# Fourier layer and maxout MLP on one core: batch 0's complex product as three float32 products, with the rows of v moved block by block and their product two groups behind

## The chip, the cores and the metric

The kernel runs on one core of one Trainium2 chip. The metric is the device time of one launch in microseconds (us), the median of several runs. Engine names are those of the profile: PE is TensorE's matmuls, PEld its weight loads, DVE is VectorE, ACT is ScalarE, POOL is GpSimd, SP is the sync engine, which here only issues transfers. An engine runs its instructions strictly in the order in which they were put on it.

## The reference

`x` is 8 batches of 3072 rows by 256 columns, float32. What must be computed, cut to what matters:

```python
X = np.fft.rfft(x, axis=1)                      # along the 3072 rows of a batch
Yr = X.real @ w_r - X.imag @ w_i + b_r          # the complex product, w_r, w_i: 256 x 256
Yi = X.real @ w_i + X.imag @ w_r + b_i
Yr = sign(Yr) * maximum(abs(Yr) - 0.01, 0)      # soft threshold, the same for Yi
y = np.fft.irfft(Yr + 1j * Yi, n=3072, axis=1)
h = maximum(maximum(y @ w1, y @ w2), y @ w3)    # 256 -> 768
out = h @ w_out                                 # 768 -> 256
```

The weights of the MLP come in as float64.

## The kernel before

A transform of 3072 points is split as 96 times 32. Stage A multiplies by a 96-point table and goes through memory (`a_d`); from there on the frequencies are taken in 12 groups (`NJP = 12`) of 128 rows and two blocks `j`. Per group k three steps on PE follow each other: `stage_b` (32-point table, tile `px`, transposed result copied to `tf`), `stage_w` (the complex product with w_r and w_i, tile `py`, result `u` with bias and soft threshold) and `stage_q` (the 32-point inverse table, tile `pz`, whose copy `zs` goes to memory as `z_d`). The last part of the inverse transform reads `z_d` back, and its result feeds the MLP, which is most of the run: 8 batches of 8 chunks, six `up`/`down` steps each.

Batches 1 to 7 run their three stages spread between the MLP's steps of the batch before. Batch 0 has no MLP to hide behind: it runs alone, before the first `up`, in plain float32, through `first_b` (line 655), `first_w` (line 682) and `first_q` (line 713). A float32 matmul shows in the trace as two instructions.

In `first_w` the rows of a group hold real and imaginary part as two halves of 64, so `tf` holds for each block the transposed pair and, in front of it, the imaginary half again with its sign turned (lines 669 and 672, two ACT copies). Each output block needs two products for each half of the 256 contracted columns: eight float32 matmuls of 128x256 a group (lines 691 and 692). Then DVE adds the bias (line 696), ACT makes two rectified copies (lines 701 and 702) and DVE subtracts them (line 703). `first_q` (line 718) takes `u` as it lies. In the loop over k (from line 1151) iteration k issues the load of group k+3, `stage_b` of k+1, `stage_w` of k and `stage_q` of k-1.

```python
for fn, i in (
    (load_a, k + 3), (stage_b, k + 1), (stage_w, k), (finish_w, k), (stage_q, k - 1),
):
```

Into the same iterations a hand-written plan (from line 1127) puts the MLP's weights: loads on SP (lines 354 and 358), and the conversion from float64 bits to two float16 halves, which is DVE and ACT work (lines 363, 390 to 409, 136 and 137). After group 11 the exponent of the largest value is taken (line 265 and on), five more float32 tiles of batch 1's stage A run on PE (line 592), `z_d` is read back (line 956), and `first_inverse` and the first `up` follow. The framework orders each engine's instructions when the program is built, by the order of the program and by when it takes operands to be ready; the order is fixed after that.

SP's queue carries the group loads (`aj`, line 629), all weights, tables and inputs; ACT's queue carries the `z_d` stores (line 894). PSUM tiles of this part come from eight banks in turn (`ff_tile`). `uf` has three buffers, `aq` two, `xm` one.

Of the kernel before, what the change touches and what calls it, by code (L numbers as in the profile page):

```python
# [101 lines left out]
def fourier_maxout_kernel(  # L102
    ctx: ExitStack, tc: tile.TileContext, x, w_r, w_i, b_r, b_i, w1, w2, w3, w_out, fa, ga, mb, mq, ident, out
):
    nc = tc.nc
# [128 lines left out]

    def load_fft_weights():
        ws = raw_tile("wst").rearrange("p (k c) -> p k c", k=KD)
        for i, w in enumerate((w_r, w_i)):
            nc.sync.dma_start(
                out=ws[:, :, i * D:i * D + D], in_=w.rearrange("(k p) d -> p k d", p=P)
            )  # L240
        return [ws[:, kd] for kd in range(KD)]

    def load_tables():
        rows = [b.rearrange("(r o d) -> r o d", r=1, o=1) for b in (b_r, b_i)]
        for c in range(2):
            nc.sync.dma_start(out=bias[64 * c:64 * c + 64, 0:1], in_=rows[c].broadcast_to([64, 1, D]))
        nc.sync.dma_start(out=qf, in_=mq[:, 0:2])
        nc.sync.dma_start(out=id_sb, in_=ident)
        st["tiled"] = s_tile("tiled")[:, 0:P]
        nc.sync.dma_start(out=st["tiled"], in_=mq[:, 26])  # L250

    def load_last_bias():
        rows = [b.rearrange("(r o d) -> r o d", r=1, o=1) for b in (b_r, b_i)]
        for c in range(2):
            nc.sync.dma_start(out=bias[64 * c:64 * c + 64, 1:2], in_=rows[c].broadcast_to([64, 1, D]))
        nc.gpsimd.dma_start(out=bias[96:97, 1:2], in_=rows[0])
# [53 lines left out]
    def scale_bias():  # L310
        mb = small("mxb")
        nc.vector.tensor_reduce(
            out=mb, in_=bias[:, 0], axis=AX.X, op=ALU.max, apply_absolute_value=True
        )
        st["eb"] = small("ebf")
        nc.vector.tensor_scalar(
            out=st["eb"], in0=exponent_of(mb, "b", 23, 0xFF, 60.0), scalar1=1.0, scalar2=-37.0,
            op0=ALU.mult, op1=ALU.add,
        )
# [185 lines left out]
    def load_m(q):  # L505
        b, q4 = divmod(q, NCH)
        xv = x[b].rearrange("(n1 n2) d -> n1 n2 d", n2=N2)[:, q4 * NQ:(q4 + 1) * NQ, :]
        with tc.issue_after(st["ld"].ins):
            st["m", q] = xm = fft.tile([N1, NQ * D], F32, name="xm", bufs=1)
            nc.sync.dma_start(out=xm.rearrange("p (n d) -> p n d", n=NQ), in_=xv)  # L510
# [147 lines left out]
    def first_b(k):  # L658
# [8 lines left out]
        st["t", k] = t = fft.tile([P, KD, 384], F32, name="tf", tag="t2", bufs=2)  # L667
        tv = t.rearrange("p h (j m) -> p (h j) m", j=2)
# [12 lines left out]

    def first_w(k):
        last = k == NJP - 1
# [3 lines left out]
        for j in range(2):  # L687
# [12 lines left out]
        t = fft.tile([P, 2, D], F32, name="t", bufs=1)  # L700
        nc.scalar.activation(out=t, in_=u, func=AF.Relu, bias=mlam)
        nc.scalar.activation(out=u, in_=u, func=AF.Relu, scale=-1.0, bias=mlam)
        nc.vector.tensor_tensor_reduce(
            out=u, in0=u, in1=t, scale=1.0, scalar=0.0, op0=ALU.subtract, op1=ALU.max,
            accum_out=mx[:, NJP + k:NJP + k + 1],
        )
# [4 lines left out]
        st["u", k] = u  # L711

    def first_q(k):
        u = st.pop(("v", k))
        pz = ff_tile("pz")
# [436 lines left out]
    for k in range(-3, NJP + 1):  # L1152
        for fn, i in (
            (load_a, k + 3), (stage_b, k + 1), (stage_w, k), (finish_w, k), (stage_q, k - 1),
        ):
            if 0 <= i < NJP:
                if fn == stage_q and i == NJP - 1:
# [4 lines left out]
        with tc.issue_after(st["ld"].ins):  # L1162
# [15 lines left out]
            if k == 6:  # L1178
                whole = ga_sb.rearrange("p i e n m -> p (i e n m)")
                nc.sync.dma_start(out=whole, in_=ga[:, 0:2 * N2 * N1])  # L1180
                first = fft.tile([N1, NQ * D], F32, name="xm", bufs=1).bitcast(F16)[:, 0:2 * NT]
# [8 lines left out]
    with tc.issue_after(st["late"].ins):  # L1190
        for c, v in enumerate((b_r, b_i)):
            row = v.rearrange("(o d) -> o d", o=1)
            nc.gpsimd.dma_start(out=bias_ri[:, c], in_=row.broadcast_to([P, D]))
# [103 lines left out]
```

## Time and profile before

| | us |
|---|---|
| median of 3 runs | 1980.62 (1979.61 to 1983.82) |
| the profiled execution's own time | 1980.65 |
| its span, first to last instruction | 1978.9 |

The profiled execution stands 0.03 us above the median, so what is worked out from its trace can be set against the median directly; 1.75 us of its time lie around the span. In the rows below, a busy time is the union of an engine's instructions; single durations overlap a little at their ends. A window's columns are its length, and for each engine the busy time and the number of instructions, then the granted share of TensorE's clock (1.00 is 2.4 GHz), the share of the 16 DMA engines in use, and GB/s.

### The profile page before, as it was taken

Reading aid. Unit: us, or ns where it says so; the run is one execution under the profiler, and the core shown is the slowest. Engines: PE = TensorE matmul, PEld = TensorE weight load, DVE = VectorE, ACT = ScalarE, POOL = GpSimd, SP = SyncE. Lnnn points to the kernel's source line nnn. Section 1 sums busy time; section 2 is a strip of 40 time slices with the busy share of each in tenths; the row PEclk is TensorE's granted clock in tenths of the full one; section 3 lists DMA queues with packets and bytes.
Section 4 is the critical chain, followed back from the end, with each engine's and each line's share of the span. In section 5 each row is a group of like instructions: output and inputs, shape, how many; then the busy total and the mean of one; then the engine's idle time right before and its main releaser. Section 6 shows DMA issues by size and latency. Waiting matters only on the chain.

```text
span 1978.9 us, 44328 instructions
## 1 busy us (share of the span) xinstructions
PE 1961.3 (99%) x16839; PEld 1355.9 (69%) x16839; DVE 1521.3 (77%) x3159; ACT 1064.3 (54%) x2186; POOL 280.5 (14%) x510
## 2 busy tenths in 40 slices
PE   9989999999999999999999999999999999999999
PEld 5746776676766766666766676666676677766666
DVE  3788887888877988778887888868887687765554
ACT  5755664566545565456554565545655455443343
POOL 1001111111111122111121021111122001100000
PEclk9999999999999999999999999999999999999999
DMA  8756564565545564555555465544552344221111
GB/s 291 212 150 172 157 163 124 156 174 154 145 133 163 143 189 115 151 150 161 159 137 149 133 186 145 147 139 130 149 154 73 90 115 123 68 76 49 49 49 33
DMA packets 201843, 269.75 MB, mean 136 GB/s; under 512 B 30846, under 2 KB 149982, under 8 KB 201534
## 3 DMA queue, kind: packets, MB, share of 16 engines
q1 hardware_dynamic: 168830, 191.37, 36.7%
q0 software_dynamic: 25168, 68.59, 10.7%
q10 hardware_dynamic: 7632, 6.95, 1.2%
q8 instruction: 133, 2.18, 0.5%
q14 instruction: 80, 0.66, 0.1%
HBM read 124.31 MB, written 75.50 MB: 101 GB/s over the span
## 4 chain that ended last, share of the span: by engine, by line
PE 93%; DVE 3%; DMA 2%; ACT 1%; issue 1%; SPq 0%; ACTq 0%; DVEq 0%
PE pu L179 19%; PE pu L181 18%; PE pu L180 18%; PE pd L181 6%; PE pd L180 6%; PE pd L179 6%; PE py L179 3%; PE py L180 3%; PE py L181 3%; PE pi L1021 2%; PE px L737 2%; PE pa L575 2%; PE pz L905 1%; PE pa L592 1%; PE py L692 0%
## 5 line engine op out<-in xcount | busy, mean ns | idle before, releaser
L179 PE MATMUL pu<-yh,wuh 128*128 128x384 f16 x2304 | 752.2, 327 | 2.6 <-DVE h L1062 1.7
L181 PE MATMUL pu<-yh,wul 128*128 128x384 f16 x2304 | 751.5, 326 | 0.0
L180 PE MATMUL pu<-yl,wuh 128*128 128x384 f16 x2304 | 751.5, 326 | 0.0
L173 ACT ACTIVATE hh<-h 128x384 f16<-128x384 f32 x384 | 200.2, 521 | 432.3 <-DVE h L1062 428.4
L181 PEld LDWEIGHTS <-wul 128*128 128x128 f16 x2304 | 225.5, 98 | 149.7 <-issue 0.9
L179 PEld LDWEIGHTS <-wuh 128*128 128x128 f16 x2304 | 225.3, 98 | 145.1 <-issue 34.2
L181 PE MATMUL pd<-woh,hh 128*128 128x256 f16 x1152 | 313.4, 273 | 0.7 <-DVE hh L174 0.7
L180 PE MATMUL pd<-wol,hh 128*128 128x256 f16 x1152 | 313.8, 273 | 0.0
L179 PE MATMUL pd<-woh,hh 128*128 128x256 f16 x1152 | 313.8, 273 | 0.0
L180 PEld LDWEIGHTS <-wuh 128*128 128x128 f16 x2304 | 225.5, 98 | 116.1 <-issue 5.0
L174 DVE SCALAR_TENSOR_TENSOR hh<-h,hh 128x384 f16<-128x384 f32 x384 | 213.3, 555 | 108.3 <-ACT hh L173 105.4
L1059 DVE TENSOR_TENSOR c<-pu,c 128x384 f32<-128x384 f32 x384 | 212.1, 552 | 95.8 <-PE pu L181 90.3
L1056 ACT ACTIVATE c<-pu 128x384 f32<-128x384 f32 x384 | 186.7, 486 | 139.9 <-PE pu L181 136.8
L1062 DVE TENSOR_TENSOR h<-pu,c 128x384 f32<-128x384 f32 x384 | 211.7, 551 | 29.2 <-PE pu L181 24.8
L1093 POOL DMA_DIRECT2D out_dram<-o x189 | 104.7, 559 | 581.3 <-ACT o L1091 569.7
L585 POOL DMA_DIRECT2D a_d<-aq x160 | 94.0, 591 | 612.4 <-ACT aq L582 590.0
L181 PE MATMUL py<-wch,tt 128*128 128x256 f16 x504 | 137.3, 273 | 0.0
L179 PE MATMUL py<-wch,tt 128*128 128x256 f16 x504 | 137.3, 272 | 0.0
L180 PE MATMUL py<-wcl,tt 128*128 128x256 f16 x504 | 137.3, 272 | 0.0
L179 PEld LDWEIGHTS <-hh 128*128 128x128 f16 x1152 | 112.7, 98 | 33.5
L180 PEld LDWEIGHTS <-hh 128*128 128x128 f16 x1152 | 112.7, 98 | 33.4
L181 PEld LDWEIGHTS <-hh 128*128 128x128 f16 x1152 | 112.7, 98 | 15.2 <-DVE hh L174 1.9
(236 smaller groups left out, 2659.3 us busy)
## 6 DMA issues: line engine op xcount, KB each, us to landing
zq<-z_d SPq DMA_DIRECT2D x63, 384.0 KB, 4.8
out_dram<-o POOLq DMA_DIRECT2D x189, 128.0 KB, 3.3
ab<-a_d SPq DMA_DIRECT2D x84, 256.0 KB, 4.1
ab<-ab SPq DMA_DIRECT2D x336, 64.0 KB, 3.0
vb<-vb SPq DMA_DIRECT2D x308, 64.0 KB, 2.9
z_d<-zs POOLq DMA_DIRECT2D x70, 256.0 KB, 3.8
xm<-in_x_dram SPq DMA_DIRECT2D x40, 384.0 KB, 3.5
a_d<-aq POOLq DMA_DIRECT2D x160, 96.0 KB, 2.9
```

The source lines that it names most:

```text
L173: nc.scalar.activation(out=hi, in_=src, func=AF.Copy, scale=scale)
L174: later(lambda: low(nc.vector.scalar_tensor_tensor(out=lo, in0=src, scalar=scale, in1=h, op0=ALU.mult, op1=ALU.subtract)))
L179: nc.tensor.matmul(o, lh, rh, start=start, stop=False, **kw)
L180: nc.tensor.matmul(o, lh, rl, start=False, stop=False, **kw)
L181: st["mm"] = nc.tensor.matmul(o, ll, rh, start=False, stop=stop, **kw)
L575: st["mm"] = nc.tensor.matmul(pa[r][64 * h:64 * h + 64], ft[rows, t], xt[rows, i, h], start=t == i, stop=t == 1,)
L585: nc.gpsimd.dma_start(out=av[1 - r, :, :, n:n + 512], in_=o[64 * h:64 * h + 48])
L737: nc.tensor.matmul(pv[:, h, :, g // 2, g % 2], ah[:, g // 2, g % 2, h * P:(h + 1) * P], mb_sb[:, i, 4 * kb + g].rearrange("p (c m) -> p c ...
L1056: st["act"] = nc.scalar.activation(out=c1, in_=p, func=AF.Copy)
L1059: st["dve"] = nc.vector.tensor_tensor(out=c1, in0=p, in1=c1, op=ALU.max)
L1062: st["dve"] = nc.vector.tensor_tensor(out=h32, in0=p, in1=st["c1"], op=ALU.max)
L1093: q.dma_start(out=out_v[b, c, t], in_=o)
```

## The change

For groups 0 to 10 of batch 0 the complex product is formed from three products: (r + i) w_r, i times -(w_r + w_i), and r times (w_i - w_r), where the first is shared by both parts of the result. The weight sums are formed once by four DVE instructions. The copies from `px` gather the real parts of both blocks into one 128-column stretch and the imaginary ones into another, DVE adds the two, and six matmuls of 128x256 follow. The result then has all 128 rows of both blocks' real part in one half and the imaginary part in the other, so the bias is added by two DVE instructions (the shared product and bias first, the rest second), and the rows have to be moved back to the layout that `first_q`'s table wants: four transfers of 64 rows by 1 KB a group on SP's queue, into half of an `aq` tile. `stage_q` runs two groups behind `stage_w` rather than one, and groups 10 and 11 both after the loop's last product. Group 11 stays as it was. The bias tile of the later batches (`bias_ri`) is loaded at the start on SP's queue (it was loaded by two POOL transfers at the end), and `xm` becomes 128 rows high, with the weight sums in columns that the table part stored there later does not use.

```diff
+    spare_x = fft.tile([P, NQ * D], F32, name="xm", bufs=1)
+    sums = spare_x[:, 2 * D:4 * D].rearrange("p (k d) -> p k d", k=KD)
+
+    def sum_fft_weights(ws):
+        for kd, t in enumerate(ws):
+            r, i, s = (t[:, n * D:n * D + D] for n in range(3))
+            nc.vector.scalar_tensor_tensor(
+                out=sums[:, kd], in0=r, scalar=-1.0, in1=i, op0=ALU.mult, op1=ALU.subtract
+            )
+            nc.vector.tensor_tensor(out=s, in0=i, in1=r, op=ALU.subtract)
...
@@ load_tables
-            nc.sync.dma_start(out=bias[64 * c:64 * c + 64, 0:1], in_=rows[c].broadcast_to([64, 1, D]))
+            nc.sync.dma_start(out=bias_ri[:, c:c + 1], in_=rows[c].broadcast_to([P, 1, D]))
@@ load_last_bias
-            nc.sync.dma_start(out=bias[64 * c:64 * c + 64, 1:2], in_=rows[c].broadcast_to([64, 1, D]))
+            nc.sync.dma_start(out=bias[64 * c:64 * c + 64], in_=rows[c].broadcast_to([64, 2, D]))
@@ scale_bias
-            out=mb, in_=bias[:, 0], axis=AX.X, op=ALU.max, apply_absolute_value=True
+            out=mb, in_=bias_ri.rearrange("p c d -> p (c d)"), axis=AX.X, op=ALU.max, apply_absolute_value=True
@@ first_b, after tf is taken
+        if k < NJP - 1:
+            pc = px.rearrange("p (h j c m) -> p h c j m", h=KD, j=2, c=2)
+            for c in range(2):
+                nc.scalar.activation(
+                    out=t[:, :, c * P:c * P + P].rearrange("p h (j m) -> p h j m", j=2), in_=pc[:, :, c],
+                    func=AF.Copy,
+                )
+            nc.vector.tensor_tensor(
+                out=t[:, :, 2 * P:3 * P], in0=t[:, :, 0:P], in1=t[:, :, P:2 * P], op=ALU.add
+            )
+            return
...
+    def quick_w(k):
+        t = st.pop(("t", k))
+        mx = batch(0, "u")
+        both = [ff_tile("py") for _ in range(2)]
+        for o, part, w in (
+            (both[0][:, 0:D], 2, [v[:, 0:D] for v in fft_weights]),
+            (both[1][:, 0:D], 1, [sums[:, h] for h in range(KD)]),
+            (both[1][:, D:2 * D], 0, [v[:, 2 * D:3 * D] for v in fft_weights]),
+        ):
+            for h in range(KD):
+                nc.tensor.matmul(
+                    o, t[:, h, part * P:(part + 1) * P], w[h], start=h == 0, stop=h == KD - 1
+                )
+        u = fft.tile([P, 2, D], F32, name="uf", tag="vh", bufs=3)
+        nc.vector.tensor_tensor(
+            out=u, in0=both[0][:, 0:D].rearrange("p (o d) -> p o d", o=1).broadcast_to([P, 2, D]),
+            in1=bias_ri, op=ALU.add,
+        )
+        nc.vector.tensor_tensor_reduce(
+            out=u, in0=both[1].rearrange("p (c d) -> p c d", c=2), in1=u, scale=1.0, scalar=0.0,
+            op0=ALU.add, op1=ALU.max, accum_out=mx[:, k:k + 1],
+        )
+        first_threshold(k, u)
+        if k % 2 == 0:
+            st["moved"] = fft.tile([P, NQ * D], F32, name="aq", bufs=2)
+        st["mv", k] = moved = st["moved"][:, k % 2 * 512:k % 2 * 512 + 512].rearrange("p (j d) -> p j d", j=2)
+        for c in range(2):
+            for j in range(2):
+                nc.sync.dma_start(out=moved[64 * c:64 * c + 64, j], in_=u[64 * j:64 * j + 64, c])
...
     def first_w(k):
+        if k < NJP - 1:
+            return quick_w(k)
...
     def first_q(k):
         u = st.pop(("v", k))
+        u = st.pop(("mv", k), u)
...
-            (load_a, k + 3), (stage_b, k + 1), (stage_w, k), (finish_w, k), (stage_q, k - 1),
+            (load_a, k + 3), (stage_b, k + 1), (stage_w, k), (finish_w, k), (stage_q, k - 2),
+            (stage_q, NJP - 1 if k == NJP else -1),
         ):
             if 0 <= i < NJP:
+                if fn == stage_w and i == 0:
+                    sum_fft_weights(fft_weights)
...
-    with tc.issue_after(st["late"].ins):
-        for c, v in enumerate((b_r, b_i)):
-            row = v.rearrange("(o d) -> o d", o=1)
-            nc.gpsimd.dma_start(out=bias_ri[:, c], in_=row.broadcast_to([P, D]))
```

`first_threshold` is the part of `first_w` from line 700 to line 706, made a function of its own.

## Rows read from the trace of the kernel before

**Rows 1.** The page's first part: busy time of each engine over the whole span, its share, and the instructions.

```profile
PE 1961.3 (99%) x16839; PEld 1355.9 (69%) x16839; DVE 1521.3 (77%) x3159; ACT 1064.3 (54%) x2186; POOL 280.5 (14%) x510
```

**Rows 2.** The windows of batch 0's own part and of the first MLP steps (columns as told above).

```profile
29.40:40.00 10.60, 9.59 (x52) 8.01 (x50) 6.92 (x24) 5.57 (x13) 0.00 (x0) 1.00 1.00 347
40.00:70.00 30.00, 29.97 (x153) 24.71 (x153) 28.62 (x64) 22.55 (x39) 0.49 (x1) 1.00 0.95 298
70.00:100.00 30.00, 27.48 (x122) 20.26 (x121) 20.41 (x62) 21.89 (x37) 1.54 (x5) 1.00 0.61 160
100.00:120.00 20.00, 16.90 (x82) 8.68 (x81) 13.49 (x24) 12.64 (x22) 2.67 (x5) 0.83 0.80 244
120.00:150.00 30.00, 26.99 (x194) 16.49 (x192) 29.62 (x61) 14.72 (x29) 0.51 (x1) 1.00 0.29 79
```

**Rows 3.** The timeline of PE over one period of the groups: start, time, instruction, and idle time before it where there was any.

```profile
49.63 0.59 PE L692 MATMUL py<-wst,tf 128*128 128x256 f32 x2
50.06 1.02 PE L718 MATMUL pz<-uf,qf 128*128 128x512 f32 x2
50.92 1.05 PE L664 MATMUL px<-mb_all,aj 128*128 128x128 f32 x8
51.81 0.60 PE L691 MATMUL py<-wst,tf 128*128 128x256 f32 x2
52.25 0.59 PE L692 MATMUL py<-wst,tf 128*128 128x256 f32 x2
...
54.84 0.59 PE L692 MATMUL py<-wst,tf 128*128 128x256 f32 x2
55.27 1.02 PE L718 MATMUL pz<-uf,qf 128*128 128x512 f32 x2
```

**Rows 4.** The timeline of DVE and ACT over what follows the product that ends at 50.2 us.

```profile
50.26 0.69 DVE L696 CUSTOM_DVE_ANT_1 uf<-py,bias 128x512 f32<-128x512 f32 x1 [0.22 <-PE py L692]
50.88 0.08 DVE L696 DVE_READ_ACCUMULATOR2_ANT mxu<- 128x1 f32 x1
51.24 0.72 ACT L701 ACTIVATE t<-uf,mlam 128x512 f32<-128x512 f32 x1
52.33 0.73 ACT L702 ACTIVATE uf<-uf,mlam 128x512 f32<-128x512 f32 x1
53.61 0.68 DVE L703 CUSTOM_DVE_ANT_0 uf<-uf,t 128x512 f32<-128x512 f32 x1
54.22 0.08 DVE L703 DVE_READ_ACCUMULATOR2_ANT mxu<- 128x1 f32 x1
```

**Rows 5.** Groups of like instructions between 27 and 130 us, different shapes apart: busy time, mean ns of one, idle time before.

```profile
L669 ACT ACTIVATE tf<-px 128x512 f32<-128x512 f32 x12 | 7.0, 586 | 14.8 <-PE px L664 11.2 <-DMA rw<-in_moe_w_out_dram 1.8 <-issue 1.0
L672 ACT ACTIVATE tf<-px 128x256 f32<-128x256 f32 x12 | 4.5, 375 | 0.0
L406 DVE SCALAR_TENSOR_TENSOR ru<-ru 128x256 f32<-128x256 uint32 x2 | 0.8, 422 | 0.0
L409 DVE TENSOR_TENSOR ru<-ru,xhl 128x256 f32<-128x256 f32 x2 | 0.8, 422 | 0.0
L312 DVE TENSOR_REDUCE mxb<-bias 128x1 f32<-128x256 f32 x1 | 0.4, 419 | 0.7 <-DMA bias<-in_b_i_dram 0.7
L303 DVE TENSOR_REDUCE mxc<-wst 128x1 f32<-128x512 f32 x2 | 1.3, 680 | 26.3 <-DMA wst<-in_w_i_dram 26.3
```

**Rows 6.** Transfers: three lines of the DMA view of 24 to 100 us (KB each, median us from issue to landing), and of the whole run the 64 KB moves of the later batches, with SP's time for the issue of one (ns, least, median, most).

```profile
rw<-in_moe_w_dram SPq DMA_DIRECT2D x6, 768.0 KB, 8.8
aj<-a_d SPq DMA_DIRECT2D x12, 256.0 KB, 6.3
z_d<-zs ACTq DMA_DIRECT2D x24, 128.0 KB, 3.2
...
vb<-vb SPq DMA_DIRECT2D x308, 64.0 KB, 2.9
...
L864 SPq DMA_DIRECT2D vb<-vb x308: 590/605/1611, 195.5 to 1733.9; - x154
```

**Rows 7.** Waits of PE between 27.2 and 100 us (us in total, times, longest), and the timeline about the longest of them.

```profile
PE pz L718 <- DVE col L265: 1.6, 1, 1.6
PE px L664 <- DMA aj<-a_d: 1.2, 2, 1.0
...
71.78 0.69 DVE L363 TENSOR_REDUCE mwd<-rw 128x2 f32<-128x512 f32 x1 [1.85 <-DMA rw<-in_moe_w_out_dram]
73.22 1.10 PE L718 MATMUL pz<-uf,qf 128*128 128x512 f32 x2 [1.62 <-DVE col L265]
```

**Rows 8.** The timeline from the last group to the first `up`.

```profile
97.33 1.13 PE L721 MATMUL pz<-uf,qf 128*128 128x256 f32 x4 [0.25 <-DVE mxu L703]
98.50 0.60 ACT L890 ACTIVATE zs<-pz 128x512 f32<-128x512 f32 x1 [0.60 <-PE pz L721]
99.12 1.24 ACTq L894 DMA_DIRECT2D z_d<-zs  x2
107.96 0.22 PE L179 MATMUL pi<-xm,zh 96*128 96x96 f16 x1 [2.41 <-ACT zh L173]
110.78 0.80 PE L179 MATMUL pu<-yh,wuh 128*128 128x384 f16 x2 [0.26 <-ACT yh L173]
```

**Rows 9.** Windows of the end of that stretch (columns as in the windows above).

```profile
108.00:110.00 2.00, 1.56 (x21) 1.42 (x22) 1.34 (x2) 0.51 (x1) 0.00 (x0) 0.56 0.68 219
112.00:114.00 2.00, 2.00 (x8) 0.95 (x7) 1.57 (x2) 0.47 (x1) 0.00 (x0) 0.50 0.88 262
115.00:116.00 1.00, 1.00 (x8) 0.57 (x7) 1.00 (x2) 0.00 (x0) 0.00 (x0) 0.97 0.95 324
```

More of the change, by code (lines that the diff above doesn't have):

```diff
@@ L508, in load_m @@
         with tc.issue_after(st["ld"].ins):
-            st["m", q] = xm = fft.tile([N1, NQ * D], F32, name="xm", bufs=1)
+            st["m", q] = xm = fft.tile([P, NQ * D], F32, name="xm", bufs=1)[0:N1]
             nc.sync.dma_start(out=xm.rearrange("p (n d) -> p n d", n=NQ), in_=xv)
@@ L680, in first_b, with first_threshold @@
                 nc.gpsimd.memset(st["ts"][:, :, z:z + 1], 0.0)
+    def quick_w(k):
[27 more added lines that the diff above has]
+                nc.sync.dma_start(out=moved[64 * c:64 * c + 64, j], in_=u[64 * j:64 * j + 64, c])
+    def first_threshold(k, u):
+        t = fft.tile([P, 2, D], F32, name="t", bufs=1)
+        nc.scalar.activation(out=t, in_=u, func=AF.Relu, bias=mlam)
+        nc.scalar.activation(out=u, in_=u, func=AF.Relu, scale=-1.0, bias=mlam)
+        nc.vector.tensor_tensor_reduce(
+            out=u, in0=u, in1=t, scale=1.0, scalar=0.0, op0=ALU.subtract, op1=ALU.max,
+            accum_out=batch(0, "u")[:, NJP + k:NJP + k + 1],
+        )
+        st["u", k] = u
     def first_w(k):
+        if k < NJP - 1:
+            return quick_w(k)
         last = k == NJP - 1
@@ L699, in first_w @@
         )
[L700 to L706, printed above, removed]
+        first_threshold(k, u)
         if last:
@@ L710, in first_w @@
             )
-        st["u", k] = u
     def first_q(k):
         u = st.pop(("v", k))
+        u = st.pop(("mv", k), u)
         pz = ff_tile("pz")
@@ L1180, in fourier_maxout_kernel @@
                 nc.sync.dma_start(out=whole, in_=ga[:, 0:2 * N2 * N1])
-                first = fft.tile([N1, NQ * D], F32, name="xm", bufs=1).bitcast(F16)[:, 0:2 * NT]
+                first = spare_x[0:N1].bitcast(F16)[:, 0:2 * NT]
                 nc.sync.dma_start(out=first, in_=ga[:, 2 * N2 * N1:])
```

## The prediction, on record before the changed kernel ran

> **What bounds the kernel now.** I read the page's busy shares first: PE is busy for 99% of the span [rows 1], so over the whole run only PE's work counts. But the change touches batch 0 alone, so next come the windows of that stretch [rows 2]. From 40 to 70 us PE is busy for 29.97 of 30 us; DVE, however, for 28.62 of the same 30, because the conversion of the MLP's weights shares the stretch. From 70 to 100 PE has 27.48 and DVE only 20.41. So the bound is PE with DVE 5% behind in the first part, and PE alone in the second. Then the timeline of PE [rows 3]: one `first_q` starts at 50.06, the next at 55.27, a period of 5.21 us without a gap; in it the product takes from 51.81 to 55.27, 3.46 us for eight matmuls, 0.43 us each. The waits [rows 7] show what else holds PE between 27 and 100 us: 1.2 us for the load of a group's rows, near the start, and 1.6 us where DVE's order put a reduction of weights that had not landed ahead of the group's work. Last the end [rows 8]: group 11's `first_q` at 97.33 releases the `z_d` round trip, and the first `up` starts at 110.78. What moves 97.33 moves all that follows.
>
> **What the change is worth, part by part.** The sum is made against the profiled execution's own 1980.65 us, which stands 0.03 above the median of 1980.62, so I set it against the median.
>
> PE: two of eight matmuls go, 2 x 0.43 = 0.86 us a group, 9.5 us over 11 groups. The period would be 4.35 us if PE still set it. That is the most that can be gained.
>
> DVE: each group gets an addition of 128x256 in SBUF, 0.42 us by its like [rows 5], and a second 128x512 addition from PSUM, for which I take the first one's 0.69; the next instruction starts 0.62 after it [rows 4], so starts stand some 0.07 closer than the durations, and the two cost 0.97 to 1.11 us a group; I take 0.97, since in a full queue it is starts that count. Eleven groups: 10.7 (12.2). The sums of the weights are four 128x256 instructions, 4 x 0.42 = 1.7, and the reduction of the bias is twice as wide, 0.68 for 0.42, +0.3. In all 12.7 us (14.2) on the engine that already had no room from 40 to 70.
>
> ACT: two copies of 128x256 in place of one of 128x512 and one of 128x256, 2 x 0.375 for 0.586 + 0.375, 0.21 us less a group. ACT is not full (22.55 of 30), so I count nothing; without that cover it would be a gain.
>
> SP and the DMA engines: four issues a group, 0.605 us each [rows 6], 2.4 us of SP a group. They wait for DVE's second threshold instruction, and behind them on SP stand the load of rows three groups ahead and the weights' loads. A group's rows are used three periods later, so I count nothing there; without that distance a late load would cost what the one in rows 7 cost, about 1 us. The bytes, 44 x 64 KB = 2.9 MB, go at 298 to 347 GB/s [rows 2], 8 to 10 us of DMA engines that are 95 to 100% in use until 70 us. What this delays is the weights (rival 3). The biases' load on SP at the start grows by 128 KB (0.4 us of transfer, beside the wait for rows), and two POOL transfers at the end go: nothing. The table part that shares its tile with the sums lies in other columns; I count nothing.
>
> The distance of two groups: from the end of a group's product to its `first_q` there are two periods. What must fit in: bias, threshold and its copies, 50.22 to 54.30 or 4.1 us [rows 3, 4]; four issues, 2.4; the landing, 2.9 us in the later batches, 6.3 for a group's rows in this crowded stretch on the same queue [rows 6]. So 9.4 to 12.8 us against 8.7 at PE's own pace and 10.4 at the old one.
>
> Now the stretch in three parts, since the limits differ.
> - 29.4 to 40 us (groups 0 and 1): DVE has 10.6 - 6.9 = 3.7 us free; it gets 1.7 + 2 x 0.97 = 3.6. No room is left, and PE's saving meets the wait for rows. I count 0, between -1.7 and +0.6.
> - 40 to 70 us: 30 / 5.21 = 5.8 groups. DVE's work becomes 28.6 + 5.8 x 0.97 = 34.2, with the bias 34.5 us; PE's falls to 25. DVE becomes the bound: **+4.5 us** (between -5.0, if the weights' work gives way entirely, and +5.4 by the full durations). The period is then about 6.0 us and the moves, which need 9.4 to 12.8 in two of them, about fit.
> - From 70 us, 3.2 groups of the new kind are left: DVE has 9.6 of 30 us free, gets 3.1, and PE sets the pace again: 3.2 x -0.86 = **-2.8 us** (0 if late weights hold it).
> - The end: group 10's rows come last now. From the end of its product 9.4 us to its `first_q`, where group 11's stands 8.4 behind it (0.86 + 3.46 + 4.1). So +1.0, and group 11's `first_q` comes another 0.86 behind: **+1.9 us**; up to 2.8 if ACT's two stores for group 10, 1.24 us [rows 8], come ahead of group 11's copy.
>
> After that nothing is added or taken. From 120 to 150 us DVE is full (29.62 of 30), so weight work that slips there would cost again, and work that slips into the 6.5 us that DVE is free from 100 to 120 would cost nothing; I count 0, with 2 us either way.
>
> Sum: 0 + 4.5 - 2.8 + 1.9 = +3.6. **Forecast: 1980.6 + 3.6 = 1984.2 us, no gain**: PE's 9.5 us are there, but where most of them fall DVE takes over the bound.
>
> A word on the moves. In this stretch a group's rows on SP's queue land in 6.3 us and the 768 KB weights in 8.8, while ACT's stores of 128 KB land in 3.2 [rows 6]. The Trainium skill (DMA: Bandwidth & Descriptors, "Queues, rings and completion order") says that each issuing engine has a ring of its own on the 16 DMA engines, and that descriptors of one ring are taken in order, those of different rings in turn. The trace agrees: what stands behind the weights is slow, what stands on the other ring is not. By that rule a move is served after all that SP issued before it, which is rival 2.
>
> **The rivals.**
> 1. PE stays the bound, faster. The weights' conversion has no due time before the first `up`; if the order put on DVE lets it slide behind the groups' work, into what is free after 70 us, the period is 4.35 from group 2 on: 9 x -0.86 = -7.7, the end +1.9: -5.8, 1974.8 us. For it: DVE has 3.7 + 1.4 + 9.6 + 6.5 = 21.2 us free from 29.4 to 120 [rows 2], and needs 12.7. Against: the plan issues the conversion ahead of later groups, and the long wait in rows 7 shows that DVE's fixed order does hold PE up. It decides if less than about 1 us of DVE time is added between two products from 40 to 70.
> 2. The moves are late, slower. With 6.3 us of landing the period is 12.8 / 2 = 6.4 until 70: 5.8 x 1.2 = +7.0; from there (4.1 + 2.4 + 2.9) / 2 = 4.7: -1.6; the end +1.9: +7.3, 1987.9 us. With the 8.8 of the weights it is 7.65 and 5.8 x 2.44 = +14.2, 1995 us. For it: the row of the crowded stretch. Against: moves are small, and the loads are ahead of need. It decides when a move takes longer than 12 - 6.5 = 5.5 us, since below that DVE hides it.
> 3. The transfers set the pace of the weights and DVE's order waits for them as at 71.78: PE's saving turns into waiting, DVE's extra work lies beside it, and the change does nothing that can be seen: 1980.6, from -2 to +3.
> 4. The clock falls. After the idle time before 107.96 the granted clock stands at 0.56 and 0.50, the 1.2 GHz level, and is back at 0.97 in the window from 115 [rows 8, 9]. If the idle parts of a DVE-bound period (6.0 - 4.35) did that, a group's PE work would be 8.7 us: 5.8 x 2.7 = +16, 2000 us. Against: the wait of 1.62 us at 71 left the window at 1.00 [rows 2, 7]. The Trainium skill (TensorE: Matmul & The Clock Gate, "Part 1: The HAM clock gate") says that too little activity halves the clock; the trace agrees at 108 us and shows no such fall among the groups.
>
> **Chances.** A difference under 0.2%, 4.0 us, is about what a measurement of this kernel cannot tell from none. The forecast 0.50, its own range 1979 to 1989 (its terms' bounds, without the two that belong to rivals); rival 1 0.20; rival 2 0.18; rival 3 0.08; rival 4 0.04. Below 1976.6: most of rival 1 and a tail of the forecast, 0.18. Above 1984.6: 0.22 of the forecast, 0.16 of rival 2, 0.01 of rival 3, rival 4: 0.43. The rest, 0.39, lies within. The range from 1975 to 1990 leaves out half of rival 1, the late end of rival 2 and rival 4, together under 0.2.
>
> **What would show it.** Right: in the changed trace PE has idle time from 40 to 70 us and its waits there name DVE; the period is near 6 us there and near 4.4 in the last groups; DVE is full until group 11. Wrong: PE full at a period of 4.35 (rival 1); PE waiting in `first_q` for the moved rows (rival 2); waits for weights in DVE's list (rival 3); a granted clock below 1.00 between 30 and 95 us (rival 4). The end is checked by two `first_q` in a row, the first waiting for a move, and by the start of the first `up`: 110.78 + 3.6 = 114.4 us. If that start has moved by the forecast and the time has not, the MLP's first steps gave it back.

## The result, and the profile after

The changed kernel takes 1998.18 us (median of 4 runs, 1997.29 to 1999.45), the kernel before 1981.74 beside it (4 runs): a ratio of 1.0085, 95% interval 1.0069 to 1.0101, so 16 us slower. The forecast was 1984.2 with a range to 1990. The profiled execution took 1997.52 us, its span is 1995.7 (1978.9 before).

The page's first part, and the windows that answer to [rows 2]:

```profile
PE 1962.6 (98%) x16795; PEld 1353.0 (68%) x16795; DVE 1532.0 (77%) x3185; ACT 1064.2 (53%) x2186; POOL 279.4 (14%) x508
```

```profile
29.40:40.00 10.60, 8.74 (x37) 7.32 (x38) 7.79 (x28) 2.92 (x7) 0.00 (x0) 0.84 0.87 306
40.00:70.00 30.00, 24.11 (x97) 18.27 (x96) 24.80 (x53) 17.74 (x32) 0.00 (x0) 0.83 0.76 222
70.00:100.00 30.00, 22.59 (x106) 16.38 (x106) 27.51 (x73) 19.39 (x33) 0.50 (x1) 1.00 0.88 249
100.00:120.00 20.00, 17.39 (x54) 9.75 (x54) 9.87 (x30) 12.46 (x22) 2.06 (x6) 0.91 0.74 218
120.00:150.00 30.00, 24.46 (x168) 14.13 (x166) 23.82 (x45) 16.50 (x31) 1.01 (x2) 0.89 0.58 174
```

No engine is full from 40 to 70 us: PE fell from 29.97 to 24.11, and DVE did not become full but fell too, from 28.62 to 24.80. The DMA engines, at 0.95 before, are at 0.76. The whole stretch waits. From 70 to 100 us DVE is at 27.51 where it was 20.41: weight work that slipped there took the room that was free before. The granted clock stands at 0.84 and 0.83 from 29.4 to 70 us, where it was 1.00, so part of the stretch ran at the 1.2 GHz level. Two of the falls came after PE had waited 2.26 us (until 43.02) and 2.12 us (until 64.39): the clock is 0.50 from 44 to 48 us and 0.53 from 66 to 68 us. Four instructions of a product then took 2.08 us, which take 1.03 at 61.24:

```profile
43.02 2.08 PE L714 MATMUL py<-xm,tf 128*128 128x256 f32 x4 [2.26 <-ACT tf L682]
```

PE's timeline about one `first_q` (answers to [rows 3]; from group 2 to group 11 the period is 6.6 us, before 5.2), then PE's waits from 27.2 to 112 us (answers to [rows 7]; us in total, times, longest):

```profile
57.90 1.06 PE L675 MATMUL px<-mb_all,aj 128*128 128x128 f32 x8
60.31 1.10 PE L776 MATMUL pz<-aq,qf 128*128 128x512 f32 x2 [1.35 <-DMA aq<-uf]
61.24 1.03 PE L714 MATMUL py<-wst,tf 128*128 128x256 f32 x4
64.39 1.16 PE L675 MATMUL px<-mb_all,aj 128*128 128x128 f32 x8 [2.12 <-DMA aj<-a_d]
65.60 1.52 PE L776 MATMUL pz<-aq,qf 128*128 128x512 f32 x2
```

```profile
PE px L675 <- DMA aj<-a_d: 6.8, 7, 2.1
PE py L714 <- ACT tf L682: 4.1, 2, 2.3
PE pz L779 <- DVE mxu L738: 2.6, 1, 2.6
PE py L714 <- DVE xm L241: 2.3, 1, 2.3
PE pz L776 <- DMA aq<-uf: 2.0, 2, 1.4
```

`first_q` (L776) waits for moved rows only 2.0 us in all; the largest entry is the groups' rows from memory, 6.8 us where it was 1.2. DVE and ACT after the product that ends at 57.85 (answers to [rows 4]):

```profile
57.56 0.68 DVE L718 TENSOR_TENSOR uf<-py,bias_ri 128x512 f32<-128x512 f32 x1
60.84 0.68 DVE L722 CUSTOM_DVE_ANT_0 uf<-py,uf 128x512 f32<-128x512 f32 x1
61.94 0.71 ACT L736 ACTIVATE t<-uf,mlam 128x512 f32<-128x512 f32 x1
62.80 0.72 ACT L737 ACTIVATE uf<-uf,mlam 128x512 f32<-128x512 f32 x1
64.51 0.68 DVE L738 CUSTOM_DVE_ANT_0 uf<-uf,t 128x512 f32<-128x512 f32 x1
```

From the product's end to the last subtraction it is 7.3 us here where it was 4.1: between the group's own steps stand weight instructions in DVE's fixed order. SP's queue from there on (start, time of the issues), and the DMA view of 24 to 100 us (answers to [rows 6]):

```profile
60.61 2.39 SPq L732 DMA_DIRECT2D aq<-uf  x4
63.05 0.59 SPq L369 DMA_DIRECT2D rw<-in_moe_w_dram  x1
...
65.78 0.59 SPq L369 DMA_DIRECT2D rw<-in_moe_w_out_dram  x1
66.48 0.41 SPq L640 DMA_DIRECT2D aj<-a_d  x1
68.15 3.99 SPq L732 DMA_DIRECT2D aq<-uf  x4
74.46 0.35 SPq L1162 DMA_DIRECT2D mb_all<-in_dft_ib_dram  x1
...
75.80 0.43 SPq L640 DMA_DIRECT2D aj<-a_d  x1
```

```profile
rw<-in_moe_w_dram SPq DMA_DIRECT2D x6, 768.0 KB, 6.4
aj<-a_d SPq DMA_DIRECT2D x12, 256.0 KB, 5.2
aq<-uf SPq DMA_DIRECT2D x38, 64.0 KB, 3.3
```

In the median the weights land sooner than before (6.4 us for 8.8), and so do the rows (5.2 for 6.3); the moves land in 3.3 us. But from the first moves on the loads are issued later: the last load of rows leaves SP at 94.62 us (67.32 before), the sixth of w1 to w3 at 63.05 (48.33). SP's own waits (24 to 112 us) name two kinds of cause for a move that could not be issued yet, a store of ACT and the threshold on DVE:

```profile
SPq L732 <- DMA z_d<-zs: 7.9, 3, 5.3
SPq L732 <- DVE mxu L738: 7.8, 4, 4.6
```

The chain of work that ended last (26 to 127 us) goes through such a store:

```profile
67.78 6.66 DMA z_d<-zs
```

It landed at 74.44; SP's issue at 74.46 had waited for it, and PE then waited for the load of rows that left behind it, at 75.80, until 80.68.

The end (answers to [rows 8]):

```profile
109.17 0.67 PE L779 MATMUL pz<-uf,qf 128*128 128x256 f32 x2 [2.61 <-DVE mxu L738]
...
110.70 1.06 PE L779 MATMUL pz<-uf,qf 128*128 128x256 f32 x2
111.98 4.56 PE L603 MATMUL pa<-xq,fr 96*96 96x512 f32 x8
126.92 0.48 PE L179 MATMUL pu<-yh,wuh 128*128 128x384 f16 x1 [0.26 <-ACT yh L173]
```

Group 11's `first_q` ends 13.3 us later (111.76 for 98.46), and the first `up` starts 16.1 us later (126.92 for 110.78), nearly the whole 16.8 us of the span. The other 2.8 us come behind group 11: of batch 1's ten `pa` matmuls two stood before its `first_q`, and now all come after it.

### The profile page after: what moved, and what is told of

It reads as the page before. It is cut to its first block, busy times and chain, and to the rows that moved or that the text cites. A ratio compares the mean times of both kernels' runs of the same rounds, so it can differ in the third digit from the quotient of the medians.

```text
span 1995.7 us, 44382 instructions
## 1 busy us (share of the span) xinstructions
PE 1962.6 (98%) x16795; PEld 1353.0 (68%) x16795; DVE 1532.0 (77%) x3185; ACT 1064.2 (53%) x2186; POOL 279.4 (14%) x508
## 3 DMA queue, kind: packets, MB, share of 16 engines
q0 software_dynamic: 25072, 68.33, 10.5%
## 4 chain that ended last, share of the span: by engine, by line
PE 91%; DMA 3%; DVE 3%; ACT 2%; issue 1%; SPq 1%; ACTq 0%; DVEq 0%
PE pu L179 18%; PE pu L181 18%; PE pu L180 18%; PE pd L181 6%; PE pd L179 6%; PE pd L180 6%; PE py L179 3%; PE py L180 3%; PE py L181 3%; PE pi L1079 2%; PE px L795 2%; PE pa L586 1%; PE pz L963 1%; PE pa L603 1%; DMA z_d<-zs 1%
```

## The experiments

The second of SP's waits above suggests a first theory (A): moves that wait for DVE stand at the head of SP's queue, and what is behind them, rows and weights, starts late. Its rivals: moved rows come too late for the distance (L, rival 2 of the prediction), the moves' bytes slow the other transfers (B), their number does, by what a transfer has to wait for on its queue (S), and DVE's additions, or the distance, cost the time (D, E). Ratios are to the kernel before in runs on the same chip, with 95% intervals.

### The parts alone

**Without moves** (`e2_no_moves`): the changed kernel, `first_q` takes `u`.

```diff
-        st["mv", k] = moved = st["moved"][...]
-        for c in range(2):
-            for j in range(2):
-                nc.sync.dma_start(out=moved[64 * c:64 * c + 64, j], in_=u[64 * j:64 * j + 64, c])
```

> The changed kernel without the 44 moves: first_q takes u as it lies, so batch 0's rows reach the inverse table in the wrong layout; all else, the distance of two groups included, stays. Theory A: 1980 to 1987 (SP is free, and only DVE's extra work and the end are left). Theory B: 1995 or above, since DVE has the same work. Theory C: as theory A, 1980 to 1987; against A it is told apart by the run with the moves on POOL.

1988.66 us, 1.0032 (1.0020 to 1.0043). The moves cost 1.0085 - 1.0032 = 0.53%, 10.5 us; all the rest 6.3.

**The moves and the distance in the kernel before** (`e3_before_moves`; four products, the four transfers put rows where `u` already had them):

```diff
+                nc.sync.dma_start(out=moved[64 * c:64 * c + 64, j], in_=u[64 * c:64 * c + 64, j])
-(stage_q, k - 1),
+(stage_q, k - 2), (stage_q, NJP - 1 if k == NJP else -1),
```

> The kernel before, with its four products, and with the moves and the distance alone: after the threshold of groups 0 to 10 four transfers on SP's queue copy u's rows to the same rows of an aq tile, and first_q runs on that copy two groups behind. Theory A: most of the loss is here without any change in PE's or DVE's work, 1990 to 2000. Theory B: 1981 to 1984. Theory C: 1985 to 1995, with PE waiting in first_q.

1997.27 us, 1.0084 (1.0060 to 1.0109): as slow as the whole change, with no product saved and no DVE work added. The profiled execution's clock is 1.00 from 29.4 to 70 us here.

**The distance alone** (`e4_before_lag2`; the second half of that diff): 

> The kernel before with first_q two groups behind and groups 10 and 11 at the end, nothing else. All three theories: 1981 to 1984, some 1 to 2 us for two first_q in a row at the end. If it is 1988 or more, the order of the stages is the cause and none of the three.

1985.01 us, 1.0009 (0.9998 to 1.0020): about 2 us, up to 4 by the interval. With it the moves alone cost the kernel before 1.0084 - 1.0009 = 0.75%.

**The three products without DVE's additions** (`e8_products_only`; the first as below, no moves), **and with distance one** (`e13_products_lag1`):

```diff
-            nc.vector.tensor_tensor(out=t[:, :, 2 * P:3 * P], in0=t[:, :, 0:P], in1=t[:, :, P:2 * P], op=ALU.add)
-        nc.vector.tensor_tensor(out=u, in0=both[0]..., in1=bias_ri, op=ALU.add)
-            out=u, in0=both[1]..., in1=u, ...
+            out=u, in0=both[1]..., in1=bias_ri, ...
```

> The three products and the distance of two alone: no moves, no sum of the two halves of tf on DVE (the shared product takes the real half in its place), no first addition (the shared product is not read, the other two are added to the bias in one instruction as in the kernel before). The output is wrong in both parts of the product. Theory D (the kernel without moves is 5 us slower than the one before because of DVE's extra 1.1 us a group): DVE's work is back at the level of before, PE's 0.86 us a group become visible in part, and the time falls to 1976 to 1983 us. Rival E (it is the distance of two and what it does to the order of the instructions that costs these 5 us): 1985 to 1989 us.

> The three products alone with stage_q one group behind as in the kernel before: no moves, no sum on DVE, no first addition (the shared product is not read and is formed from the real half), so the output is wrong in both parts. It is the most that the change could give. Theory D (distance two costs 1 to 3 us at the end and at the start, PE's saving is real): 1976 to 1981 us, that is 3 us or more below the same kernel with distance two (1984.0). Rival E (transfers pace this stretch, so PE's saving turns into waits for loads whatever the distance): 1981 to 1984 us.

1983.97 us, 1.0016 (1.0003 to 1.0029), and 1986.26 us, 1.0029 (1.0017 to 1.0040). DVE's additions cost 0.0032 - 0.0016 = 0.16%, 3 us, with intervals that overlap a little, so this price is at the edge of the noise. But even without them the three products gain nothing: PE waits for `tf`, for `col` and for rows instead (4.2, 2.5 and 2.3 us in the second run). The first time lies between the ranges of theories D and E, the second above both: the gain that D expected did not come, and putting the distance back to one did not bring it.

### What of the moves costs: first tries

**On POOL's queue** (`e1_moves_pool`; `nc.sync` becomes `nc.gpsimd` in the move): 

> The changed kernel with the 44 moves issued on POOL's queue in place of SP's; nothing else differs. Theory A (SP's order: the moves wait on SP for DVE and hold up the loads of rows, weights and inputs that stand behind them): the loads come as early as before the change, PE's 6.8 us of waits for a group's rows go, the time falls by 8 us or more, to 1990 or below. Theory B (DVE's extra work sets the pace, as I predicted): nothing changes but a few tenths, 1996 to 2000. Theory C (the moved rows themselves come late): 1996 to 2000 too, since the way of the rows is as long on either queue.

2001.26 us, 1.0099 (1.0079 to 1.0119). PE's waits for rows fell to 0.9 us, and 14.1 us of waits for moved rows came, so theory A's 1990 was not reached.

**On POOL, three groups behind** (`e5_pool_three_behind`; `stage_q` at k - 3, three moved tiles): 

> The changed kernel with the 44 moves issued on POOL's queue, the last bias row taken off POOL so that between stage A's stores and the copy for group 11 POOL holds moves alone, and stage_q three groups behind stage_w (three moved tiles in place of two). The output is the reference's. Theory A (the moves cost only as a wait: on SP they hold the loads behind them, on POOL they came too late for a distance of two): nothing stands behind a waiting move now and the rows have a period more to land, so PE's wait in first_q for moved rows falls from 14.1 us to under 3, the wait for group loads stays under 2, and the time is that of the kernel without moves plus a period's share at the end: 1988 to 1991 us. Rival C (the moves' own bytes, 2.9 MB, or their issue slow the other transfers wherever they are issued): the first_q wait is small, but the time stays at 1995 to 2000 us. Rival P (POOL's issue itself is late by several us a move): the first_q wait stays over 8 us and the time near 2000.

1996.33 us, 1.0070 (1.0048 to 1.0093); PE still waited in `first_q`, up to 5.6 us at a time. None of the three expectations met it whole.

**Rows loaded five groups ahead** (`e9_loads_ahead`; `load_a` at k + 5): 

> The changed kernel with its moves on SP as they are, but the groups' rows loaded five groups ahead from iteration 3 on (two of them in iterations 0 and 2 each) and not three, into the same buffers. The output is the reference's. Theory A1 (of what stands behind the waiting moves only the groups' rows matter): PE's wait for them falls from 6.8 us to under 1.5 and the time to 1989 to 1992 us. Theory A2 (weights and inputs behind the moves matter as much, through DVE's order, or the rows that come late are only the first to be missed): the wait for rows goes, others take its place, and the time stays at 1994 to 1998 us. Rival C (bytes): no change, 1997 to 1999 us.

2000.54 us, 1.0088 (1.0069 to 1.0108). The waits for rows went (1.2 us), waits for moved rows took their place (15.6): A2.

**Moves from a ready source** (reading `tf`, tile unread, `first_q` takes `u`): the same moves on SP (`e7_ready_moves`), on POOL (`e10_pool_ready`), 4 rows each on SP (`e11_small_on_sp`), one transfer per group on SP (`e12_one_transfer`).

```diff
-  in_=u[64 * j:64 * j + 64, c]
+  in_=tt[64 * j:64 * j + 64, c, 0:D]
```

> The changed kernel with the same 44 moves at the same places of SP's queue, of the same size and into the same tiles, but read from tf, which stands ready before the product, and not from u; first_q takes u as it lies, so its rows are in the wrong layout. Theory A (SP's fixed order: a move waits for DVE at the head of the queue, and loads of rows, weights and inputs behind it start late): a move finds its source ready, SP is not held up, PE's wait for group loads falls from 6.8 us to under 2.5, and the time is that of the kernel without moves and up to 2 us more: 1988 to 1991 us. Rival C (bytes and issue time of the moves): 1995 to 1999 us. Half way, 1992 to 1994, would share it between both.

> The changed kernel with the same 44 moves of the same size into the same tiles, but issued on POOL's queue, read from tf, which stands ready before the product, and read by nobody: first_q takes u as it lies (its rows are in the wrong layout), and the last bias row goes to SP's queue. So the bytes are moved in the same stretch, but no engine waits for a moved row, and the moves take no place among the transfers of SP and ACT. Theory B (the bytes fill the DMA engines and slow the loads and stores beside them): 1993 to 1999 us. Theory S (the moves cost by their place on SP's queue, where each transfer waits until the one eight places before it on SP and ACT together has landed; on POOL they cost only as rows that come late): 1987 to 1990.5 us, as the kernel without moves, with PE's waits for group loads under 3 us.

> The changed kernel with its 44 moves at the same places of SP's queue, read from tf, which is ready early, but of 4 rows (4 KB) and not 64 rows each; first_q takes u as it lies, in the wrong layout. So nearly no bytes are moved (0.18 of 2.9 MB), nothing waits for DVE, but each group still issues four transfers more on SP, each of which waits until the transfer eight places before it on SP and ACT has landed. Theory S (places and issues): the loads of the groups' rows stay as late as in the changed kernel, PE's waits for them stay over 4 us, and the time is 1994 to 1999 us. Theory B (bytes): SP runs ahead as without moves, the waits for rows are under 2.5 us and the time is 1987 to 1991 us.

> The changed kernel with each group's four moves as one transfer of the same 256 KB in the same 1 KB rows, from tf to the same tile, 128 rows straight across (no row changes its partition), at the same place of SP's queue; nobody reads it, and first_q takes u as it lies, in the wrong layout. The bytes are all there, but the group takes one place and one issue on SP in place of four. Theory S (places and issues): 1988 to 1992 us, the rows' loads early again. Theory B (bytes): 1994 to 1999 us.

1999.25 us, 1.0082 (1.0061 to 1.0103); 1999.24, 1.0099 (1.0078 to 1.0121); 1998.20, 1.0088 (1.0073 to 1.0103); 1995.18, 1.0073 (1.0055 to 1.0090). In the first, a move that waits for no engine costs as much, which speaks against theory A. The four don't settle it, since ACT's next copy into `tf` has to wait until the moves have read it, and stands later in ACT's order: in the third, `px` of group 3 was there at 42.5 us and its copy began at 45.18, behind four weight instructions.

### What of the moves costs: sources that hold nobody up

In these nobody reads the moved tile, and no tile in the chain of a group but `u` (three buffers) is touched.

**Constant source on SP** (`e14_constant_moves`), **source `u` on SP** (`e15_unread_moves`), **source `u` on POOL** (`e16_pool_unread`):

```diff
-  nc.sync.dma_start(out=moved[64 * c:64 * c + 64, j], in_=u[64 * j:64 * j + 64, c])
+  nc.sync.dma_start(out=moved[64 * c:64 * c + 64, j], in_=fft_weights[c][64 * j:64 * j + 64, 0:D])
```

> The changed kernel with the 44 moves of the same size at the same places of SP's queue, but read from the Fourier weights, a constant that is there from 31 us on, and written into tiles that nobody reads; first_q takes u as it lies, in the wrong layout. No move waits for an engine, nobody waits for a move. Theory A (a move that waits for DVE at the head of SP's queue holds the loads) and theory L (first_q waits for rows that come late): both costs are gone, 1988 to 1991 us, as the kernel without moves. Theory B (the bytes in the DMA engines, and that a transfer of SP waits for the one eight places before it on SP and ACT): 1994 to 1999 us, with the loads of rows as late as in the changed kernel.

> The changed kernel with its moves on SP as they are, from u, but nobody reads the moved tiles: first_q takes u as it lies, in the wrong layout. A move still waits for DVE at the head of SP's queue; no engine waits for moved rows. Theory L (the loop over first_q: from a product's end to its moved rows some 13 us, two periods of 6.6): 1988 to 1991 us. Theory A (SP held): 1994 to 1999 us, with PE's waits for group loads over 4 us. Theory B (bytes): 1994 to 1999 us too, and then the run with a constant source is as slow.

> The changed kernel with the 44 moves from u on POOL's queue (the last bias row on SP's) into tiles that nobody reads; first_q takes u as it lies, in the wrong layout. The instructions of PE and DVE stand in the order of the kernel without moves, and SP's queue carries what it carries there. What is left of the moves are 2.9 MB through the DMA engines, and POOL's own work to issue them. Theory A and theory L: 1987 to 1990 us, no slower than the kernel without moves by more than 2 us. Theory B (bytes): 1993 to 1999 us, with loads that land later.

2000.29 us, 1.0104 (1.0087 to 1.0121); 1998.70, 1.0094 (1.0079 to 1.0109); 1996.29, 1.0080 (1.0065 to 1.0095). So neither the wait for DVE at the head of SP's queue (A) nor `first_q`'s wait for moved rows (L) is needed for what the moves cost; transfers that nobody wants cost as much.

How they do it on POOL shows best in the third, where PE, DVE and ACT have the order of the kernel without moves. SP's queue carries one transfer more there, the last bias row, which was POOL's; it waited 4.0 us. The DMA view of 24 to 100 us, and two of the waits from 27 to 112 us (DVE's and PE's), without moves:

```profile
q1 hardware_dynamic: 8640, 15.49, 62.6%
...
aj<-a_d SPq DMA_DIRECT2D x12, 256.0 KB, 6.9
rw<-in_moe_w_out_dram SPq DMA_DIRECT2D x2, 512.0 KB, 4.1
```

```profile
DVE mwd L374 <- DMA rw<-in_moe_w_out_dram: 0.2, 1, 0.2
...
PE px L675 <- DMA aj<-a_d: 1.8, 3, 0.8
```

With the moves:

```profile
q1 hardware_dynamic: 8642, 15.49, 66.5%
q0 software_dynamic: 1249, 2.57, 12.2%
...
aj<-a_d SPq DMA_DIRECT2D x12, 256.0 KB, 8.4
rw<-in_moe_w_out_dram SPq DMA_DIRECT2D x2, 512.0 KB, 11.6
```

```profile
DVE mwd L374 <- DMA rw<-in_moe_w_out_dram: 8.0, 2, 5.9
...
PE px L675 <- DMA aj<-a_d: 6.2, 5, 3.0
```

The moves (q0) took 12.2% of the 16 engines' 76 us, 9.3 us for 2.57 MB. The loads on SP (q1) carry the same 15.49 MB in both, and land later: w_out's in 11.6 us for 4.1. DVE then waits for w_out, PE for rows. How much of this is the bytes' doing, the runs with 4 rows below tell.

On SP the same moves have a second way to cost, one that stands in the program and not in the bytes: each transfer of SP and of ACT takes the next of eight completion semaphores, and before it is issued it waits until the transfer that had this semaphore before has landed. From the list of SP's instructions with their waits, constant source:

```
72 L1243 DMA ga_sb_78<-in_dft_ia_dram 96x6144 [waits DMAHW1_49]
73 L1245 DMA xm_87<-in_dft_ia_dram 96x768 [waits DMAHW4_49]
74 L640 DMA aj_625<-a_d_139 128x2x256 [waits DMAHW5_49,PE_49]
75 L732 DMA aq_608<-wst_227 64x256 [waits DMAHW7_49]
76 L732 DMA aq_608<-wst_227 64x256 [waits DMAHW0_49]
77 L732 DMA aq_608<-wst_227 64x256 [waits DMAHW1_49]
```

SP's waits in that run's trace (27 to 106 us) show it:

```profile
SPq L732 <- DMA z_d<-zs: 10.2, 4, 7.2
SPq L732 <- DMA ga_sb<-in_dft_ia_dram: 3.9, 1, 3.9
SPq L369 <- DMA rw<-in_moe_w_dram: 3.0, 2, 2.2
```

A move whose source is a constant and whose target nobody reads waits 3.9 us for `ga_sb`, and 7.2 us for a store of ACT, with which it shares no data. Behind it stand the loads of rows and weights. Four moves a group take four of eight places. Without moves SP waits for ACT's stores too, once for 8.3 us, but the sixth load of w1 to w3 has left by then, at 45.11 us.

**4 rows in place of 64**, on POOL (`e17_pool_small`) and, from the constant, on SP (`e18_sp_small`):

```diff
-  moved[64 * c:64 * c + 64, j], in_=u[64 * j:64 * j + 64, c]
+  moved[64 * c:64 * c + 4, j], in_=u[64 * j:64 * j + 4, c]
```

> As the run with unread moves from u on POOL's queue, but each of the 44 moves carries 4 rows (4 KB) and not 64: POOL's work and the number of transfers are the same, 0.18 MB go through the DMA engines in place of 2.9; the instructions of PE and DVE stand in the order of the kernel without moves. The output's rows are in the wrong layout as there. Theory B (on POOL the bytes cost, by slowing the loads where the DMA engines are full): 1987 to 1990.5 us, as the kernel without moves. Rival N (the number of transfers, or POOL's work beside DVE): 1994 to 1997 us, no less than with 64 rows.

> As the run with moves from a constant source on SP, unread, but each of the 44 moves carries 4 rows (4 KB) and not 64. No move waits for an engine, nobody waits for a move, and nearly no bytes are moved; first_q takes u as it lies, in the wrong layout. Theory S (on SP the places cost: each transfer waits until the one eight places before it on SP and ACT has landed, and the moves take about half of the places): 1994 to 2000 us, the group loads issued as late as in the changed kernel. Theory B (the bytes cost): 1988 to 1991 us. Between them, 1991 to 1994, both have a share.

1990.67 us, 1.0052 (1.0037 to 1.0067), and 1994.65 us, 1.0074 (1.0057 to 1.0091): the first just above theory B's range, the second inside theory S's. Taking the bytes away gives back 0.28% on POOL and 0.30% on SP, 5.5 and 6 us, with intervals that just touch. What stays above the kernel without moves is 0.20% on POOL, where the intervals overlap too, and 0.42% on SP, where they don't. The waits follow the bytes only in part. On POOL with 4 rows (same windows as above):

```profile
rw<-in_moe_w_out_dram SPq DMA_DIRECT2D x2, 512.0 KB, 9.0
```

```profile
DVE mwd L374 <- DMA rw<-in_moe_w_out_dram: 3.1, 1, 3.1
...
PE px L675 <- DMA aj<-a_d: 5.3, 4, 3.3
```

DVE's wait for w_out falls with the bytes, from 8.0 to 3.1 us; PE's wait for rows hardly does, 5.3 for 6.2, where it is 1.8 without moves. In this run too the bias row on SP waited, 3.9 us, with the loads behind it. On SP with 4 rows the sixth load of w1 to w3 leaves at 59.23 us and the last of the rows at 90.45, against 45.11 and 75.33 without moves. So the bytes have a share on either queue, and on SP something that is not the bytes has another.

**Half of the moves** (`e19_half_moves`; the two blocks that lie on the right partitions are copied by POOL):

```diff
-            for j in range(2):
-                nc.sync.dma_start(out=moved[64 * c:64 * c + 64, j], in_=u[64 * j:64 * j + 64, c])
+            nc.sync.dma_start(out=moved[64 * c:64 * c + 64, 1 - c], in_=u[64 - 64 * c:128 - 64 * c, c])
+            nc.gpsimd.tensor_copy(out=moved[64 * c:64 * c + 64, c], in_=u[64 * c:64 * c + 64, c])
```

> The changed kernel with two moves a group on SP in place of four: the two blocks of u that already lie on the partitions where they are wanted are copied into the moved tile by POOL (two copies of 64x256 a group). The output is the reference's. Half of the moves' bytes and half of their places are gone. If bytes and places are the cause, whichever it is, half of the 10 us goes: 1991 to 1995 us, and the group loads are issued earlier than in the changed kernel. If what costs is that first_q depends on a moved row at all, or that a move waits for DVE on SP, it stays at 1996 to 1999 us.

1994.28 us, 1.0068 (1.0053 to 1.0083): a third of the moves' price is gone, inside the expected 1991 to 1995, though the interval still overlaps that of the whole change. It is no clean half: PE's wait for rows fell to 1.8 us, but `first_q` now waited 5.7 us for moves and 4.1 for POOL's copies. No version came near the kernel before.

| kernel | ratio to before |
|---|---|
| distance two alone | 1.0009 (0.9998 to 1.0020) |
| changed, no moves, no DVE additions | 1.0016 (1.0003 to 1.0029) |
| changed, no moves | 1.0032 (1.0020 to 1.0043) |
| POOL, 4 rows, unread | 1.0052 (1.0037 to 1.0067) |
| half of the moves on SP | 1.0068 (1.0053 to 1.0083) |
| SP, 4 rows, constant, unread | 1.0074 (1.0057 to 1.0091) |
| POOL, 64 rows, unread | 1.0080 (1.0065 to 1.0095) |
| the kernel before, with moves and distance two | 1.0084 (1.0060 to 1.0109) |
| the change | 1.0085 (1.0069 to 1.0101) |
| SP, 64 rows from `u`, unread | 1.0094 (1.0079 to 1.0109) |
| SP, 64 rows, constant, unread | 1.0104 (1.0087 to 1.0121) |

## Why the prediction was wrong

- **The step that failed is the one on SP and the DMA engines.** "A group's rows are used three periods later, so I count nothing there." The term counted at 0 measured 10.5 us. The step had worked out the price of the bytes, 8 to 10 us of DMA engines that were 95 to 100% in use, and then booked it to the weights alone, as rival 3, which could only eat PE's gain. Measured, the bytes are worth 5.5 to 6 us of time, on POOL mostly through w_out. The other share, 0.42% or 8 us with 4 KB moves on SP, is put down here to the places on SP's queue: the step looked for what a move waits for (DVE) and not for what every transfer waits for (the one with its semaphore before it). That these waits happen, on the chain too, the traces show; that they are the whole of this share is not shown (see what stays open). The distance of three periods to a load's use holds from the moment it is issued; with the moves that moment came later, for the last rows at 94.62 us, where it is 75.33 without moves.
- **DVE becomes the bound from 40 to 70 us, +4.5.** Not seen: with late loads DVE is at 24.80 of 30 us there. Without moves it is at 26.05, and the time is up by 6.3 us where the forecast's sum without any price for moves said +3.6. The sign held, the size was 3 us short: DVE's additions cost about 3 us, and the -2.8 for PE's pace after 70 us did not come: DVE, which was to have 9.6 us free there, is at 28.83 of 30 us without moves.
- **PE's 0.86 us a group** are not visible in any run, not even with the products alone. Rival 1 (1974.8) has no run that speaks for it. Which wait would have to go first was not settled.
- **The distance and the end, +1.9.** Distance two alone cost about 2 us (from none to 4 by its interval), which agrees with the count. In the changed kernel the stretch behind group 11 is 2.8 us longer besides; the step did not look at the `pa` matmuls.
- **Rival 2 (moves late)** had the right side and the wrong place: its sign was to be PE waiting in `first_q`, which is 2.0 us. From a product's end to its `first_q` it did take longer than the 9.4 us, 10 to 18 in groups 0 to 6 (57.85 to 75.55 in group 4), and of that the 4.1 us became 6 to 7 from group 1 on. But with rows that nobody waits for the time is the same. Its point of decision, a move slower than 5.5 us, was not reached either: 3.3. The rule of the Trainium skill that was weighed there (DMA: Bandwidth & Descriptors, "Queues, rings and completion order") made a move slow behind SP's weights; here the moves landed in 3.3 us, in the median, beside weights in 6.4 on the same queue, and what delayed them was their issue, of which that rule says nothing.
- **Rival 4 (the clock)** was at 2000 us, near the result, and its sign was seen: the clock fell to 0.83. It is not needed for the loss, but it may carry a share of it. What the granted clock leaves missing of full clock, added up from 28 to 150 us in steps of 2 us, is 12.0 us in the changed kernel's profiled execution and 3.4 in the one before; so by this estimate at most 8.6 of the 16.9 us between them, about half, go with the clock, and at most 3.4 without moves, where 6.8 are missing. On the other side, the kernel before with moves and distance misses 5.1 and took 1995.98 us in that execution. The run with unread moves on POOL misses 5.1 as well, stands at 1.00 from 29.4 to 70 us, and took 1993.97; the one without moves stands at 0.84 and 0.94 there and took 1989.09. In the changed kernel PE's waits come first, and the clock falls behind them. The windows of the run on POOL:

```profile
29.40:40.00 10.60, 8.34 (x42) 6.48 (x42) 9.22 (x32) 2.92 (x7) 1.08 (x2) 1.00 0.94 328
40.00:70.00 30.00, 24.27 (x117) 18.24 (x118) 26.85 (x63) 19.82 (x37) 9.34 (x19) 1.00 0.95 305
```

What stays open: on SP the program also puts instructions of DVE, ACT and PE in another order when moves are there, and no run parts that from the places; whether POOL's 44 issues, or the bias row that went to SP's queue with them, cost anything beside the bytes (1.0052 against 1.0032); and how much of the loss the clock carries.

## What to carry to other kernels

Count transfers as a load of their own, in bytes and in number, where the DMA engines are nearly full, as here (0.95 to 1.00 in use before): 44 moves of 64 KB that nobody waited for left this kernel 16 to 20 us above the one before; without them it was 6. Ask of every queue how many transfers may be under way before the next is held, and who shares these places: small ones take as many as large ones, and 44 of 4 KB on SP, from a constant, still left it about 14 us above. And a test of "it only costs by its wait" is the same work with nobody waiting.

## What was not expected of the hardware and the program

- The 64 KB moves took 9.3 us of all 16 DMA engines for 2.57 MB on POOL's queue, 277 GB/s; the loads of that stretch without moves (q1) took 62.6% of 76 us, 47.6 us, for 15.49 MB, 326 GB/s.
- A move of 4 KB on POOL's queue landed hardly faster in this stretch than one of 64 KB: 5.1 and 5.8 us in the median.
- SP and ACT share eight completion semaphores in this program, so a late store of ACT held SP's transfers: 7.2 us in one wait with moves from a constant, 8.3 in one without moves.
